# An FNet–GLU layer on one core: x laid out by tiles, early high parts made from raw x, sums and means added by accumulating transfers, and late side work at other places

## The chip, the core and the metric

The kernel runs on one core of a Trainium2 chip. A core has TensorE (PE in the profile: matmuls; PEld is its loading of weights), VectorE (DVE), ScalarE (ACT), GpSimd (POOL) and SyncE (SP). Two queues of transfers matter: SP issues the loads from DRAM ("hardware" transfers), POOL issues the stores and all transfers that add onto their target ("software", accumulating transfers). The metric is the device time of one execution in microseconds (us); a measurement is the median of several runs.

## The reference, cut to what matters

x is [1, 2048, 512], all in fp32.

```python
xn = layernorm(x)                               # over the 512 columns, no weights
a, b = xn @ Dhid_re.T, xn @ Dhid_im.T           # 512 x 512
s = Dseq_re @ a - Dseq_im @ b                   # 2048 x 2048
g = silu((sigmoid(xn @ w_gate) * (xn @ w_up)) @ w_down)   # 512 -> 1792 -> 512
out = x + s * g
```

## The kernel before

**Numbers.** Each fp32 matmul is three TensorE passes over fp32r operands. An operand v is split into a *high* part (ScalarE copies v into an fp32r tile, L118 or L356) and a *low* part (VectorE subtracts the high part from v, L123 or L359); the passes are high·high, high·low and low·high. An operand that takes part in a matmul therefore costs ScalarE about one pass over it and VectorE another.

**Products.** Every large matrix product is done as 2×2 blocks with seven block products instead of eight, which needs sums of blocks (`combine`, L127, on VectorE). For the sequence DFT, the stationary side comes from x (`a_sums`) and the moving side from the DFT matrices (`onto`, L228: t1 = c_re block + c_im block, and so on). Since the real part only is kept, the sequence DFT is made first (real columns of c_re and c_im), and the hidden DFT afterwards.

**Units.** TensorE's work is a list of 245 units in a fixed order. Units 0 to 111 are the sequence DFT: four chunks of 512 output rows (t = 0 to 3), seven products each, four tiles of x (pp = 0 to 3) each, 12 matmuls in a unit. The first 24 units take products 1 and 2 of chunks 0, 1 and 2 in turn, so that one tile of x serves three units: unit 0 needs the first tile, unit 3 the second, unit 6 the third, unit 9 the fourth. Units 112 to 209 are the GLU: 14 blocks of seven units, with 12 matmuls of gate and up and, after the first block, 6 of the down projection. Units 210 to 244 are the hidden DFT, with what was left of the down projection; there silu(g) is multiplied in and the result added onto `out`.

**What sets the order.** The order is written out by hand: `sooner(n, f)`, `amid(n, f)` and `after(n, f)` hang a piece of side work f before, in the middle of, or behind unit n. For each unit the program issues, in this order, the `sooner` work, the loads for this unit and the next five, the high and low parts for this unit and the next two, the `amid` work, the unit's matmuls, the `after` work. Each engine and each queue takes its own instructions in the order in which they are issued.

```python
for k in range(n, min(n + LOAD_AHEAD + 1, len(units))):   # LOAD_AHEAD = 5
    for p in units[k][0]:
        p.load()
ahead = [p for _, (ps, _) in zip(range(SPLIT_AHEAD + 1), units[n:]) for p in ps]   # SPLIT_AHEAD = 2
```

**Pages.** Everything in the core's memory, raw blocks, parts, sums and results alike, lies in 54 pages of 4 KB a partition that are given out in rotation. A new page has to wait until the last reader of its former content is done; where that reader is a store to DRAM, until the store has landed.

**The start** (`begin`, L409). 14 matmuls on a tile of ones run first. x and the first block of c_re come in as two halves each. `stats` (L165) makes mean and variance of a row on VectorE and 1/sqrt(variance + eps) on GpSimd (L175 for 128x1, L178 for 128x2), then −mean on VectorE (L181) and −mean/sigma on GpSimd (L184). `normed` (L351) subtracts and scales on VectorE, `high` copies on ScalarE, `low` subtracts on VectorE. The other half of the columns of a tile is normalised by ScalarE in place (`normalise`, L187). The odd rows of the tiles (j = 1) are treated the same way around units 4 to 16.

**The GLU's x.** The GLU takes a transposed x from the host (x_t) and normalises it in the kernel: `store_moments` (L192) writes −mean and 1/sigma of each block of 512 tokens to DRAM (m_part), and `x_norm` (L462) broadcasts them back to all partitions and, for each of 8 tiles, adds the mean and multiplies by 1/sigma on VectorE (L475, 16 instructions of 128x1024). They hang on units 76 to 97 and 121 to 137.

**Other side work.** `f_sums` (L691) and `w_sums` (L711) make the block sums for the hidden DFT and store them in DRAM (f_sum, w_part). `Seven` holds a GLU block's gated values; its four sums hang on units n+7 to n+10 of a block that begins at n. A block's down projections are stored or added onto g_part in DRAM (`keep`, L515). `put_x` (L737) copies x_t into `out` by seven transfers from DRAM to DRAM, hung on units 40, 48, … 96.

Of the kernel before, what the change touches and what calls it, by code (L numbers as in the profile page):

```python
# [14 lines left out]
P = 128  # L15
# [7 lines left out]
SB = 512  # L23
# [9 lines left out]
def fnet_glu_kernel(ctx: ExitStack, tc: tile.TileContext, x, x_t, c_re, c_im, w_h, w_gu, w_down, out):  # L33
# [18 lines left out]
    nc.gpsimd.memset(mhalf, -0.5)  # L52
    warm = const.tile([P, 2], F32, name="warm")
    nc.scalar.activation(warm, mhalf, AF.Sigmoid)
    moments = const.tile([P, 4, 3, 2, 2], F32, name="moments")
    m_part = [dram.tile([P, 2, 4], F32, name=f"m_part{i}") for i in range(NT)]
# [92 lines left out]
    def fetch(j, pp, e=None):  # L149
        if (j, pp) not in xs:  # L150
            xs[j, pp] = page([2, D], F32)
        if pp == 0:
            rows = x[:SB, :].rearrange("(e j p) d -> j p e d", j=2, e=2)[j]
        else:
            rows = x[pp * SB : (pp + 1) * SB, :].rearrange("(p j e) d -> j p e d", j=2, e=2)[j]
        if e is None and pp:
            nc.sync.dma_start(xs[j, pp], rows)
        else:
            for i in range(2) if e is None else (e,):
                nc.sync.dma_start(xs[j, pp][:, i, :], rows[:, i, :])  # L160

    def moment(pp, m, j):
        return moments[:, 0, m, :, j] if pp == 0 else moments[:, pp, m, j, :]

    def stats(j, pp, apart=None):  # L165
        mv = stat.tile([P, 2, 2], F32, name="mv")
        rs = stat.tile([P, 2], F32, name="rs")
        mean, scale, bias = (moment(pp, m, j) for m in range(3))
        for e in range(2):
# [3 lines left out]
            if apart:  # L173
                nc.vector.tensor_scalar(rs[:, e : e + 1], mv[:, e, 1:2], EPS, None, op0=ALU.add)
                nc.gpsimd.tensor_tensor(scale[:, e : e + 1], rs[:, e : e + 1], mhalf[:, e : e + 1], op=ALU.pow)  # L175
        if not apart:
            nc.vector.tensor_scalar(rs, mv[:, :, 1], EPS, None, op0=ALU.add)
            nc.gpsimd.tensor_tensor(scale, rs, mhalf, op=ALU.pow)  # L178
        if apart:
            apart(mv, 0)  # L180
        nc.vector.tensor_scalar(mean, mv[:, :, 0], -1.0, None, op0=ALU.mult)  # L181
        if apart:
            apart(mv, 1)
        nc.gpsimd.tensor_tensor(bias, mean, scale, op=ALU.mult)  # L184
        return mv
# [6 lines left out]
    def store_moments(b):  # L192
        nc.gpsimd.dma_start(m_part[b], moments[:, b, 0:2].rearrange("p m a b -> p m (a b)"))
# [31 lines left out]
    def c_block(t, pp, j, m):  # L225
        return Load((c_re, c_im)[m][t, j, pp], [2, SB])
# [134 lines left out]
    def prepare(pp, between=None):  # L361
        parts, src = tile_of(pp)

        def step(mv, e):
            normed(pp, mv, e)
            high(parts, src, e)
            if between:
                between(e)
# [594 lines left out]
```

## Time and profile before

| | |
|---|---|
| median of 3 runs | 802.24 us (801.84 to 802.99) |
| the profiled execution | 802.94 us, of which span 801.2 us |
| TensorE clock granted | full in every slice |
| PE busy | 789.2 us (99%), 3470 matmuls |
| DVE busy | 691.5 us (86%), 905 instructions |
| ACT busy | 511.9 us (64%), 783 instructions |
| POOL busy | 118.9 us (15%), 163 instructions |
| transfers | 174.72 MB, mean 218 GB/s |

All times are of one profiled execution. "Busy" is the time that an engine had an instruction in work; matmuls overlap, and a group of n matmuls shown as one row lasts from the start of its first to the end of its last. Behind "<-" stands what an engine had been waiting for. Start times count from the start of the span.

### The profile page before, as it was taken

How to read it: one execution, taken by the hardware profiler on the slowest of the kernel's cores; microseconds unless marked ns; L12 is line 12 of the kernel's file. 1: busy time of each engine (PE TensorE's matmuls, PEld its weight loads, DVE VectorE, ACT ScalarE, POOL GpSimd, SP SyncE). 2: the span in 40 equal slices, each digit the busy share in tenths (PEclk: the TensorE clock that was granted, in tenths of full speed). 3: DMA queues.
4: the chain of work that ended last, by engine and by line, in shares of the span. 5: the costliest groups of instructions: out<-in, count | busy, mean ns of one | idle time of the engine just before them, and what ended most of it. 6: DMA issues, size and time to landing. Idle time of an engine off the chain costs nothing.

```text
span 801.2 us, 9892 instructions
## 1 busy us (share of the span) xinstructions
PE 789.2 (99%) x3470; PEld 649.5 (81%) x3470; DVE 691.5 (86%) x905; ACT 511.9 (64%) x783; POOL 118.9 (15%) x163
## 2 busy tenths in 40 slices
PE   8999999999999999999999999999999999999997
PEld 7787888888878888888887887878888888888886
DVE  7999999688899898899999967869688898896957
ACT  5795655535434455677778776566577787887571
POOL 1321001001110000011111111222131111112201
PEclk9999999999999999999999999999999999999999
DMA  9954065396897336138976885899999798999996
GB/s 337 418 200 174 1 247 200 126 340 233 299 412 296 105 132 213 51 129 220 200 129 92 176 174 169 258 259 243 241 263 214 158 229 224 223 290 300 296 346 106
DMA packets 49617, 174.72 MB, mean 218 GB/s; under 512 B 5536, under 2 KB 5792, under 8 KB 49568
## 3 DMA queue, kind: packets, MB, share of 16 engines
q0 software_dynamic: 20320, 70.28, 40.2%
q1 hardware_dynamic: 29168, 103.76, 35.4%
q8 instruction: 27, 0.44, 0.2%
q14 instruction: 22, 0.18, 0.1%
q10 hardware_dynamic: 80, 0.07, 0.0%
HBM read 106.95 MB, written 70.80 MB: 222 GB/s over the span
## 4 chain that ended last, share of the span: by engine, by line
PE 74%; DVE 13%; issue 5%; DMA 4%; ACT 1%; POOL 1%; SPq 0%; DVEq 0%; POOLq 0%; ACTq 0%
PE pd L70 21%; PE ga L70 13%; PE ua L70 13%; PE gc L70 9%; PE uc L70 9%; DVE page L123 6%; PE gb L70 5%; PE ub L70 5%; DVE page L127 4%; DMA g_part<-page 2%; DMA w_part<-page 2%; DVE page L475 1%; DMA page<-in_c_re_dram 1%; DVE st L171 1%; DVE page L652 1%
## 5 line engine op out<-in xcount | busy, mean ns | idle before, releaser
L118 ACT ACTIVATE page<-page 128x1024 fp32r<-128x1024 f32 (+1 forms) x381 | 301.7, 831 | 153.6 <-DVE page L127 128.8
L123 DVE TENSOR_TENSOR page<-page 128x1024 fp32r<-128x1024 f32 (+1 forms) x381 | 347.1, 943 | 55.9 <-ACT page L118 54.2
L70 PE MATMUL pd<-page 128*128 128x512 f32 (+1 forms) x984 | 238.3, 387 | 0.5 <-ACT page L526 0.5
L70 PEld LDWEIGHTS pd<-page 128*128 128x128 f32 x984 | 183.0, 188 | 38.7 <-ACT page L526 1.0
L127 DVE TENSOR_TENSOR page<-page 128x1024 f32<-128x1024 f32 (+2 forms) x252 | 205.0, 836 | 5.9 <-DMA page<-in_w_gu_dram 5.1
L70 PE MATMUL ga<-page 128*128 128x512 f32 x600 | 156.8, 391 | 4.0 <-DVE page L123 1.8
L70 PE MATMUL ua<-page 128*128 128x512 f32 x600 | 155.5, 389 | 0.0
L70 PEld LDWEIGHTS ga<-page 128*128 128x128 f32 x600 | 112.0, 188 | 30.5 <-ACT page L634 2.7
L70 PEld LDWEIGHTS ua<-page 128*128 128x128 f32 x600 | 112.6, 188 | 23.5
L70 PE MATMUL gc<-page 128*128 128x512 f32 x408 | 106.7, 389 | 0.0
L70 PE MATMUL uc<-page 128*128 128x512 f32 x408 | 106.6, 389 | 0.0
L517 POOL DMA_DIRECT2D g_part<-page x76 | 65.4, 860 | 277.8 <-ACT page L526 160.0
L526 ACT ACTIVATE page<-pd 128x512 f32<-128x512 f32 x140 | 81.8, 600 | 26.2 <-PE pd L70 17.7
L70 PEld LDWEIGHTS gc<-page 128*128 128x128 f32 x408 | 76.5, 188 | 16.1 <-DVE page L123 0.3
L70 PEld LDWEIGHTS uc<-page 128*128 128x128 f32 x408 | 76.6, 188 | 15.9
L70 PE MATMUL gb<-page 128*128 128x512 f32 x228 | 61.1, 390 | 0.2 <-DVE page L123 0.2
L70 PE MATMUL ub<-page 128*128 128x512 f32 x228 | 61.0, 389 | 0.0
L70 PEld LDWEIGHTS gb<-page 128*128 128x128 f32 x228 | 42.6, 188 | 9.6 <-DVE page L123 0.8
L70 PEld LDWEIGHTS ub<-page 128*128 128x128 f32 x228 | 42.8, 188 | 8.9
L294 POOL DMA_DIRECT2D f_raw<-page x16 | 8.7, 542 | 207.1 <-DVE page L306 145.2
L652 DVE TENSOR_TENSOR page<-page 128x512 f32<-128x512 f32 x28 | 19.4, 691 | 8.7 <-ACT page L649 7.9
L612 DVE TENSOR_TENSOR page<-page,pd 128x512 f32<-128x512 f32 x28 | 18.5, 684 | 6.9 <-PE pd L70 6.9
(86 smaller groups left out, 357.2 us busy)
## 6 DMA issues: line engine op xcount, KB each, us to landing
g_part<-page POOLq DMA_DIRECT2D x84, 512.0 KB, 7.1
page<-in_c_re_dram SPq DMA_DIRECT2D x47, 512.0 KB, 8.2
page<-in_c_im_dram SPq DMA_DIRECT2D x32, 512.0 KB, 6.8
page<-f_raw SPq DMA_DIRECT2D x28, 512.0 KB, 8.8
page<-in_w_gu_dram SPq DMA_DIRECT2D x22, 512.0 KB, 6.5
f_raw<-page POOLq DMA_DIRECT2D x16, 512.0 KB, 5.3
f_sum<-page POOLq DMA_DIRECT2D x16, 512.0 KB, 7.2
page<-f_sum SPq DMA_DIRECT2D x16, 512.0 KB, 12.5
```

Of the source, the lines that this page charges most:

```text
L70: nc.tensor.matmul(ps, ws[w], ms[m], start=first and i == 0, stop=last and i == 2, skip_group_check=go_on)
L118: nc.scalar.activation(self.parts[0], self.raw, AF.Copy)
L123: nc.vector.tensor_tensor(lo, self.raw, hi.bitcast(F32), op=SUB)
L127: (engine or nc.vector).tensor_tensor(dst, a, b, op=op)
L171: nc.vector.bn_stats(st, xs[j, pp][:, e, :])
L294: nc.gpsimd.dma_start(f_raw[self.t][block], v)
L475: nc.vector.tensor_tensor(to, to, by, op=(ADD, ALU.mult)[m])
L517: nc.gpsimd.dma_start(g_part[i], pg, accum_op=ADD)
L526: nc.scalar.activation(pg[:, o, :], po, AF.Copy, scale=float(sign))
L612: nc.vector.tensor_add(self.part[:, o, :], self.part[:, o, :], ps)
L652: nc.vector.tensor_mul(s[k][:, 0, :], s[k][:, 0, :], ps["u" + tag] if tag else s[k][:, 1, :])
```

## The change

1. **Layout.** The host lays x out as one contiguous block for each tile and j. The block of tile 0, and the first c_re block of chunks 0 and 1, are laid out as two contiguous halves. The special order of c_re for tile 0 is gone.
2. **Start.** 13 warming matmuls for 14. `normed` is now ScalarE's: for the first half of a tile's columns one instruction makes the high part straight from raw x, and a second one normalises x in place, from which VectorE subtracts the high part; VectorE's subtract-and-scale (L353) and its −mean (L181) are gone. In exchange GpSimd has three small steps for each set of statistics (−mean, power, −mean/sigma) for two. For the third and fourth tile the statistics hang one unit earlier (units 3 and 6) and are made for both rows at once. The order of the matmuls inside units 0 and 3 is another one. `stats(1, pp)` hangs on units 6, 8, 10, 13 (before on 4, 7, 10, 13), its `normalise` on 8, 10, 13, 16 (before 7, 10, 13, 16), and `a_sums` steps 3, 2, 4 on 20+pp, 22+pp, 28+pp (before 10+3pp, 13+3pp, 17+5pp).
3. **Class `Sum`.** For chunk 0, the sums t1 and t3 (eight in all) are not added by VectorE; the c_im block is added onto the loaded c_re or c_im page by an accumulating transfer of POOL's queue.
4. **`x_norm`.** The mean is added onto the raw tile by an accumulating transfer that broadcasts m_part, five units before the multiplication; the raw tile is loaded nine units before it. Only the multiplication is left on VectorE (L501 in the changed kernel, 8 instructions), on units 82, 85, 88, 94 and 122, 125, 129, 132.
5. **Later places.** `w_sums` from unit 158 to 174, `f_sums(1, 1)` from 178 to 182, `put_x` from units 40 to 96 to units 114 to 126, `x_ops(1)` from units 139–150 to 134–150, and the fourth sum of `Seven` from before a unit's loads (n+10) to the middle of unit n+9.

The diff, cut to its core:

```diff
+        def scale(e):
+            mean, by, bias = (moment(pp, m, j)[:, e] for m in range(3))
+            nc.vector.tensor_scalar(rs[:, e], mv[:, e, 1], EPS, None, op0=ALU.add)
+            nc.gpsimd.tensor_tensor(mean, mv[:, e, 0], minus[:, e], op=ALU.mult)
+            nc.gpsimd.tensor_tensor(by, rs[:, e], mhalf[:, e], op=ALU.pow)
+            nc.gpsimd.tensor_tensor(bias, mean, by, op=ALU.mult)
+
             if apart:
-                nc.vector.tensor_scalar(rs[:, e : e + 1], mv[:, e, 1:2], EPS, None, op0=ALU.add)
-                nc.gpsimd.tensor_tensor(scale[:, e : e + 1], rs[:, e : e + 1], mhalf[:, e : e + 1], op=ALU.pow)
+                scale(slice(e, e + 1))
         if not apart:
-            nc.vector.tensor_scalar(rs, mv[:, :, 1], EPS, None, op0=ALU.add)
-            nc.gpsimd.tensor_tensor(scale, rs, mhalf, op=ALU.pow)
-        if apart:
-            apart(mv, 0)
-        nc.vector.tensor_scalar(mean, mv[:, :, 0], -1.0, None, op0=ALU.mult)
-        if apart:
-            apart(mv, 1)
-        nc.gpsimd.tensor_tensor(bias, mean, scale, op=ALU.mult)
-        return mv
+            scale(slice(0, 2))
...
     def store_moments(b):
-        nc.gpsimd.dma_start(m_part[b], moments[:, b, 0:2].rearrange("p m a b -> p m (a b)"))
+        for m in range(2):
+            nc.gpsimd.dma_start(m_part[b][m], moments[:, b, m].rearrange("p a b -> p (a b)"))
...
-        return Load((c_re, c_im)[m][t, j, pp], [2, SB])
+    class Sum(Value):
+
+
+        def __init__(self, base, more):
+            super().__init__([base], None)
+            self.base, self.more = base, more
+
+        def load(self):
+            if self.at is None:
+                self.at = self.base.load()
+                nc.gpsimd.dma_start(self.at, self.more.src, accum_op=ADD)
+
+        def get(self):
+            self.load()
+            return self.at
...
-                t1 = Value([b11, b12], onto(b11.load, b12.load))
+                t1 = Value([b11, b12], onto(b11.load, b12.load)) if t else Sum(b11, b12)
                 t2 = Value([b22], onto(t1.get, b22.load))
-                t3 = Value([b22], onto(b12.load, b22.load))
+                t3 = Value([b22], onto(b12.load, b22.load)) if t else Sum(b12, b22)
...
                 if (self.t, k, pp) == (0, 1, 0):
-                    turns.sort(key=lambda v: v[1])
+                    turns.sort(key=lambda v: (v[1], (0, 2, 1).index(v[2][0])))
+                elif (self.t, k, pp) == (0, 1, 1):
+                    turns.sort(key=lambda v: (v[2] == (2,), v[1], v[2]))
                 elif (k, pp) == (1, 0):
                     turns.sort(key=lambda v: (v[2], v[1]))
...
-            total = (9, 6) if self.t == 0 and k == 5 else (6, 3)
+            total = (9, 3) if self.t == 0 and k in (5, 7) else (6, 3)
...
-    def normed(pp, mv, e):
-        v = a_block(0, 0, pp)[:, e]
-        nc.vector.tensor_scalar(v, v, mv[:, e, 0:1], moment(pp, 1, 0)[:, e : e + 1], op0=SUB, op1=ALU.mult)
+    def normed(pp, to, src, e):
+        nc.scalar.activation(to[:, e], src[:, e], AF.Identity, scale=moment(pp, 1, 0)[:, e : e + 1], bias=moment(pp, 2, 0)[:, e : e + 1])
...
+        for e in range(2):
+            normed(pp, parts[0], src, e)
+        for e in range(2):
+            normed(pp, src, src, e)
...
                     sooner(m - 11, lambda pp=pp: fetch(1, pp))
-                    after(m - 8, lambda pp=pp: stats(1, pp))
-                    after(m - 5, lambda pp=pp: normalise(1, pp))
+                    after((6, 8, 10, 13)[pp], lambda pp=pp: stats(1, pp))
+                    after((8, 10, 13, 16)[pp], lambda pp=pp: normalise(1, pp))
                 else:
                     if pp > 1:
+                        sooner(m - 3, lambda pp=pp: stats(0, pp))
                         sooner(m - 2, units[m][0][1].high)
                         sooner(m - 2, lambda pp=pp: ready.append(prepare(pp)))
                         amid(m - 2, lambda: low(*ready.pop()))
...
-            after(m - 2, lambda pp=pp: a_sums(pp, (3,)))
+            after(20 + pp, lambda pp=pp: a_sums(pp, (3,)))
             after(m - 1, aop[5, pp].get)
-            after(m + 1, lambda pp=pp: a_sums(pp, (2,)))
-            after(m + 5 + 2 * pp, lambda pp=pp: a_sums(pp, (4,)))
+            after(22 + pp, lambda pp=pp: a_sums(pp, (2,)))
+            after(28 + pp, lambda pp=pp: a_sums(pp, (4,)))
...
-            for _ in range((4, 4, 3, 3)[i]):
+            for _ in range((4, 4, 3, 2)[i]):
...
+        first, second = (chunks[t].op[1, 0] for t in range(2))
+        for c in (first, second):
+            c.raw = c.loads[0].at = page([2, SB], F32)
+            c.parts = page([2, SB]), page([2, SB])
+            for e in range(2):
+                nc.sync.dma_start(c.raw[:, e, :], c.loads[0].src[:, e, :])
         fetch(0, 1)
-        for n in (3, 4):
+        for n in (2, 3, 4):
             units[n][0][1].load()
         fetch(0, 2)
         units[5][0][1].load()
-        c.at = page([2, SB]), page([2, SB])
-        a, first = prepare(0, lambda e: high(c.at, raw.at, e))
+        stats(0, 0, True)
+        a, src = tile_of(0)
         for e in range(2):
-            low(a, first, e)
-            low(c.at, raw.at, e)
-        units[1][0][1].get()
+            high(first.parts, first.raw, e)
+            normed(0, a[0], src, e)
+            normed(0, src, src, e)
+            low(first.parts, first.raw, e)
+            low(a, src, e)
+        first.at = first.parts
+        for e in range(2):
+            high(second.parts, second.raw, e)
+        second.get()
+        units[2][0][1].high()
+        stats(0, 1, True)
+        a, src = tile_of(1)
+        normed(1, a[0], src, 0)
+        normed(1, src, src, 0)
         units[2][0][1].get()
+        low(a, src, 0)
         units[3][0][1].high()
-        a, second = prepare(1)
-        low(a, second)
+        normed(1, a[0], src, 1)
+        normed(1, src, src, 1)
+        units[3][0][1].get()
+        low(a, src, 1)
 
...
-        def step(j, m):
+        def centre(j):
+            nc.gpsimd.dma_start(raw[j].load(), mean.unsqueeze(1).to_broadcast([P, 2, SB]), accum_op=ADD)
+
+        def step(j):
             v = xraw[h, j, b] = raw[j].load()
-            by = both.load()[:, :, m, :]
-            if c == 0:
-        sooner(at[0] - 5, both.load)
-        for i in range(4):
-            if i % 2 == 0:
-                sooner(at[i] - 5, raw[i // 2].load)
-            after(at[i], lambda i=i: step(*divmod(i, 2)))
+            nc.vector.tensor_tensor(v, v, by.load().unsqueeze(1).to_broadcast([P, 2, SB]), op=ALU.mult)
+
+        sooner(at[0] - 5, by.load)
+        for j in range(2):
+            sooner(at[j] - 9, raw[j].load)
+            after(at[j] - 5, lambda j=j: centre(j))
+            after(at[j], lambda j=j: step(j))
...
             for i, v in enumerate(self.sums):
-                sooner(n + 7 + i, v.get)
+                (amid if i == 3 else sooner)(n + (7, 8, 9, 9)[i], v.get)
...
         n = len(units)
-        x_norm(0, 0, (n - 36, n - 33, n - 30, n - 27))
-        x_norm(0, 1, (n - 24, n - 21, n - 18, n - 15))
+        x_norm(0, 0, (n - 30, n - 27))
+        x_norm(0, 1, (n - 24, n - 18))
...
-        x_norm(1, 0, (n + 9, n + 12, n + 15, n + 18))
-        x_norm(1, 1, (n + 21, n + 22, n + 24, n + 25))
-        x_ops(1, (n + 27, n + 28, n + 29, n + 30, n + 31, n + 32, n + 33, n + 34, n + 35, n + 36, n + 38))
+        x_norm(1, 0, (n + 10, n + 13))
+        x_norm(1, 1, (n + 17, n + 20))
+        x_ops(1, (n + 22, n + 24, n + 26, n + 27, n + 28, n + 30, n + 32, n + 33, n + 35, n + 36, n + 38))
-        f_sums(1, 1, n + 66, 1)
-        w_sums(n + 46)
+        f_sums(1, 1, n + 70, 1)
+        w_sums(n + 62)
+        for i, (pair, k) in enumerate(itertools.product(range(NT // 2), BLOCK)):
+            if (pair, k) != LAST:
+                after(n + 2 + 2 * i, lambda pair=pair, k=k: put_x(pair, *BLOCK[k]))
```

In the rows below, `ga`, `ua` and so on are accumulators in PSUM, `page` is any page, `st`, `mv`, `rs` and `moments` hold the statistics, and the number behind an L is the line of the kernel that the rows are of (L123 and L127 before are L125 and L129 in the changed kernel, L171 is L178, L359 is L376).

VectorE at the third tile of x (needed by unit 6), from its statistics to its low part, before:

```order
L171 BN_STATS st<-page 128x6
L172 BN_AGGR mv<-st 128x2
L174 TENSOR_SCALAR rs<-mv 128x1
L353 TENSOR_SCALAR page<-page,mv,moments 128x256
L181 TENSOR_SCALAR moments<-mv 128x2
L353 TENSOR_SCALAR page<-page,mv,moments 128x256
L123 TENSOR_TENSOR page<-page 128x1024
L359 TENSOR_TENSOR page<-page 128x512
```

and in the changed kernel (the row of `rs` is L171 there):

```order
L178 BN_STATS st<-page 128x6
L179 BN_AGGR mv<-st 128x2
L171 TENSOR_SCALAR rs<-mv 128x2
L125 TENSOR_TENSOR page<-page 128x1024 x2
L376 TENSOR_TENSOR page<-page 128x512
L125 TENSOR_TENSOR page<-page 128x1024
```

Between the statistics and the low part stand two subtractions of other operands now, one before; the two L353 are gone from VectorE.

GpSimd at the same tile and the next set of statistics, before:

```order
L175 TENSOR_TENSOR moments<-rs,mhalf 128x1 x2
L184 TENSOR_TENSOR moments<-moments 128x2
L178 TENSOR_TENSOR moments<-rs,mhalf 128x2
L184 TENSOR_TENSOR moments<-moments 128x2
```

and in the changed kernel, for one set, with the first transfers that follow the last set:

```order
L172 TENSOR_TENSOR moments<-mv,minus 128x2
L173 TENSOR_TENSOR moments<-rs,mhalf 128x2
L174 TENSOR_TENSOR moments<-moments 128x2
L192 DMA m_part0a<-moments 128x4
L192 DMA m_part0b<-moments 128x4
L238 DMA page<-in_c_im_dram 128x1024 x3
```

Three steps stand where two or three stood, and the accumulating transfers of `Sum` (L238) share the queue with the stores of the moments.

VectorE around units 76 to 82, before (L306 is `join`, L475 is `x_norm`):

```order
L475 TENSOR_TENSOR page<-page 128x1024
L127 TENSOR_TENSOR page<-page 128x1024
L123 TENSOR_TENSOR page<-page 128x1024
L127 TENSOR_TENSOR page<-page 128x1024 x2
L123 TENSOR_TENSOR page<-page 128x1024
L127 TENSOR_TENSOR page<-page 128x1024
L123 TENSOR_TENSOR page<-page 128x1024
L306 TENSOR_TENSOR page<-page,pd 128x512 x2
L475 TENSOR_TENSOR page<-page 128x1024
L127 TENSOR_TENSOR page<-page 128x1024 x2
L123 TENSOR_TENSOR page<-page 128x1024 x2
```

and in the changed kernel (`join` is L324, the multiplication L501):

```order
L125 TENSOR_TENSOR page<-page 128x1024
L324 TENSOR_TENSOR page<-page,pd 128x512 x2
L129 TENSOR_TENSOR page<-page 128x1024 x2
L125 TENSOR_TENSOR page<-page 128x1024 x2
L129 TENSOR_TENSOR page<-page 128x1024
L125 TENSOR_TENSOR page<-page 128x1024
L501 TENSOR_TENSOR page<-page 128x1024
```

The two L475, the additions of unit 76 and the multiplication of unit 79, are gone from this place; the first multiplication stands behind unit 82, at the end of these rows.

71 lines of the change are left out of this document (28 added, 43 removed).

## The prediction

> **What bounds the kernel now.** I read the page first.
>
> ```profile
> PE 789.2 (99%) x3470; PEld 649.5 (81%) x3470; DVE 691.5 (86%) x905; ACT 511.9 (64%) x783; POOL 118.9 (15%) x163
> PE 74%; DVE 13%; issue 5%; DMA 4%; ACT 1%; POOL 1%; SPq 0%; DVEq 0%; POOLq 0%; ACTq 0%
> ```
>
> TensorE is busy for 99% of the span, and the change takes one of the warming matmuls from it and nothing else. Only 801.2 − 789.2 = 12 us of the span are without a matmul: the time before the first one, the last store, and waits in between. The next view is the list of what PE waited for.
>
> ```profile
> PE ga L70 <- DVE page L123: 1.8, 1, 1.8
> PE ga L70 <- ACT page L634: 1.3, 2, 0.8
> PE ga L70 <- ACT page L356: 0.6, 1, 0.6
> PE pd L70 <- ACT page L526: 0.5, 1, 0.5
> PE ga L70 <- DVE page L359: 0.3, 1, 0.3
> PE gb L70 <- DVE page L123: 0.2, 1, 0.2
> ```
>
> Beside the first matmul's (the 0.6) these are 4.1 us in six waits. A wait costs more than its row; PE's timeline shows it for the longest.
>
> ```profile
> 230.74 1.52 PE L70 MATMUL ua<-page 128*128 128x512 f32 x6
> 232.10 0.61 PE L70 MATMUL ga<-page 128*128 128x512 f32 x2
> 234.47 1.20 PE L70 MATMUL ga<-page 128*128 128x512 f32 x4 [1.76 <-DVE page L123]
> 235.51 1.54 PE L70 MATMUL ua<-page 128*128 128x512 f32 x6
> ```
>
> Six matmuls take 232.10 − 230.74 = 1.36 us, 0.227 each; a unit of 12 takes 2.72, a GLU unit of 18 takes 4.08. From 232.10 to 234.47 are 2.37 us for two matmuls (0.45), so 1.92 are lost, and the four behind them take 1.04 for 0.91, 0.13 more. The wait of 1.76 cost 2.05, that is 0.28 above its row.
>
> **Where the waits come from.** First VectorE ahead of this one, and the window's busy times (PE, PEld, DVE, ACT, POOL; then clock, DMA share, GB/s).
>
> ```profile
> 217.72 2.10 DVE L475 TENSOR_TENSOR page<-page 128x1024 f32<-128x1024 f32 x1
> 228.89 2.13 DVE L475 TENSOR_TENSOR page<-page 128x1024 f32<-128x1024 f32 x1
> 233.21 2.42 DVE L123 TENSOR_TENSOR page<-page 128x1024 fp32r<-128x1024 f32 x2
> ```
>
> ```profile
> 220.00:240.00 20.00, 18.24 (x81) 14.77 (x80) 20.00 (x18) 6.93 (x8) 2.87 (x5) 1.00 1.02 412
> ```
>
> VectorE had no free moment in this window (20.00 of 20.00), and PE was released when the first of the two subtractions ended. Two additions or multiplications of `x_norm` (4.23 us) had been put in ahead of it. It is a backlog of VectorE, not a missing load. Then ScalarE in the GLU, and two steps of the chain of waits there:
>
> ```profile
> 434.99 0.63 ACT L118 ACTIVATE page<-page 128x512 fp32r<-128x512 f32 x1 [2.55 <-issue]
> 493.93 0.60 ACT L634 ACTIVATE page<-ga 128x512 f32<-128x512 f32 x1 [0.63 <-DVE page L123]
> 526.17 1.09 ACT L526 ACTIVATE page<-pd 128x512 f32<-128x512 f32 x2 [2.47 <-DMA w_part<-page]
> ```
>
> ```profile
> 480.15 7.06 DMA g_part<-page
> 513.72 12.37 DMA w_part<-page
> ```
>
> At 435 ScalarE stood for 2.55 us, and its snapshot of PSUM (L634), for which PE waits, came behind it. I put that to VectorE, which was busy there with `x_norm`'s last instructions and the sums of `x_ops(1)`. At 494 and 526 a page was still on its way to DRAM when ScalarE wanted to fill it again: behind the loads of `w_sums` (unit 154 on) a store of g_part took 7.06 us, and the store of w_part 12.37.
>
> **The sum, part by part.**
>
> *Middle of the kernel: −4.7 us.* Of the two L475 ahead of 233.21 one addition is gone altogether and one multiplication stands behind unit 82, the unit that waited; VectorE has 4.2 us less to do there and was 1.9 late. In the second stretch, eight instructions become four and stand from unit 122 to 132 instead of 121 to 137; `w_sums` leaves units 154 to 161. So all four waits go: 1.8 + 1.3 + 0.5 from the list and 4 × 0.28 = 1.1 for the restarts, 4.7. The bounds are −2.0 (only the wait at 234) and −4.7.
>
> *What pays for it.* Each mean is now an accumulating transfer. The rows are the landing of the nearest such group (accumulations onto g_part, L517), and the loads of x_t around 200 to 260 us:
>
> ```profile
> DMA to landing us min/median/max: 5.1/7.2/15.0
> ```
>
> ```profile
> page<-in_x_t_dram SPq DMA_DIRECT2D x4, 512.0 KB, 7.6
> ```
>
> Raw load and accumulation follow each other, 14.8 us by the medians; from the load, nine units ahead, to the multiplication are 9 × 2.72 = 24.5 us. Hidden, so nothing; with the longest landing 22.6 us, and it still holds. The seven copies of `put_x` leave the sequence DFT, which makes room on the same transfer engines.
>
> *Sums of chunk 0: nothing by themselves.* Eight additions leave VectorE:
>
> ```profile
> L127 DVE TENSOR_TENSOR page<-page 128x1024 f32<-128x1024 f32 x76 | 92.3, 1221 | 0.0
> ```
>
> 8 × 1.22 = 9.8 us. The transfers are issued nine units ahead of their own unit and the split begins two units ahead, so there are 7 × 2.72 = 19 us; t1 only accumulates (7.2, at most 15.0), t3 loads first (14.8 together, 22.6 with the longest). Taken as hidden; the bound is 3.6 us once.
>
> *Start: −0.6 us.* The rows of GpSimd's power and multiplication, the first matmul, and ScalarE's normalisation of half a tile:
>
> ```profile
> 4.82 0.57 POOL L175 TENSOR_TENSOR moments<-rs,mhalf 128x1 f32<-128x1 f32 x1 [3.98 <-DVE rs L174]
> 6.49 0.20 POOL L184 TENSOR_TENSOR moments<-moments 128x2 f32<-128x2 f32 x1
> 7.01 0.50 PE L70 MATMUL ga<-page 128*128 128x512 f32 x1 [0.62 <-ACT page L356]
> ```
>
> ```profile
> L190 ACT ACTIVATE page<-page,moments 128x256 f32<-128x256 f32 x8 | 4.3, 593 | 0.0
> ```
>
> First matmul: 4.82 + 0.20 + 0.57 + 0.20 + 0.59 and 0.1 of handing on give 6.5 for 7.01, −0.5. In the second half of unit 0 ScalarE has two normalisations and one copy to do again, some 1.6 us for 1.36 of matmuls, and VectorE a subtraction behind them: +0.4. The second tile waits for the same chain once more, +0.2 (0 to 1.3). For the third tile:
>
> ```profile
> 19.41 0.69 DVE L171 BATCH_NORM_STATS2 st<-page 128x6 f32<-128x512 f32 x1
> 23.73 0.68 DVE L359 TENSOR_TENSOR page<-page 128x512 fp32r<-128x512 f32 x1
> 24.33 0.69 DVE L171 BATCH_NORM_STATS2 st<-page 128x6 f32<-128x512 f32 x1
> 26.07 0.17 DVE L177 TENSOR_SCALAR rs<-mv 128x2 f32<-128x2 f32 x1
> 52.28 2.96 DVE L123 TENSOR_TENSOR page<-page 128x1024 fp32r<-128x1024 f32 x3
> ```
>
> ```profile
> 26.32 1.67 POOL L178 TENSOR_TENSOR moments<-rs,mhalf 128x2 f32<-128x2 f32 x1 [3.81 <-DVE moments L181]
> 52.39 1.17 POOL L184 TENSOR_TENSOR moments<-moments 128x2 f32<-128x2 f32 x1
> ```
>
> Before, from statistics to low part took 24.41 − 19.41 = 5.0 us. Now: both rows' statistics 26.24 − 24.33 = 1.9; three steps of GpSimd; four activations of ScalarE, 4 × 0.54 = 2.1 (4.3 / 8 of the row above); the subtraction 0.69. GpSimd's multiplication takes 0.20 alone and took 1.17 while VectorE ran its subtractions (it ended at 53.56, as the first of the three at 52.28 did): it is held by them. So its three steps take from 0.20 + 2 × 0.57 + 0.20 = 1.5 us to 1.17 + 1.67 + 1.17 = 4.0, and the order puts two subtractions right behind the statistics. The chain makes 6.2 to 8.7 for 5.0; it begins a unit (2.72) earlier. That leaves −1.5 to +1.0; I take +0.5, nearer the upper end, because the subtractions stand at that very place. [...] The fourth tile:
>
> ```profile
> 32.60 0.63 PE L70 MATMUL ua<-page 128*128 128x512 f32 x2
> 33.55 0.73 PE L70 MATMUL ga<-page 128*128 128x512 f32 x2 [0.32 <-DVE page L359]
> ```
>
> 0.95 for two matmuls that take 0.45, 0.8 lost there with the pairs beside it; its statistics now start a unit earlier, and the additions that crowded VectorE come later: −0.6. The 0.2 of the list (at 70.4, 0.6 with what follows it) was VectorE's backlog, and 9.8 us are gone: −0.6. In all −0.5 + 0.4 + 0.2 + 0.5 − 0.6 − 0.6 = −0.6, from −2.3 (nothing given back, the later tiles as now or better) to +1.3 (second tile 1.3, third 1.0).
>
> *`w_sums` at its new place: +0.8 us.* Now it is at units 170 to 177, where these stand:
>
> ```profile
> 560.00:580.00 20.00, 20.00 (x90) 16.57 (x89) 12.31 (x18) 11.56 (x20) 3.40 (x4) 1.00 0.93 248
> 580.00:600.00 20.00, 20.00 (x90) 16.57 (x89) 16.12 (x23) 14.76 (x27) 6.46 (x9) 1.00 1.00 252
> 600.00:620.00 20.00, 20.00 (x90) 16.57 (x89) 17.16 (x29) 15.62 (x27) 3.20 (x4) 1.00 0.95 218
> ```
>
> PE loses nothing there today (20.00), but the transfer engines have little left. In the rotation of pages, the changed program reuses at units 168 to 169 pages that were sent to DRAM only two units (8.2 us) before; the closest ones of before were one to three units, at units 155 to 164, where it cost the two waits. A store lands in 7.2 us by the median and 15.0 at most: 0 to 2.2 us (what the two waits at 494 and 526 cost), and I take 0.8, since two units are more than the median.
>
> *Without effect on the end:* the layout as such (the loads are ahead of their use except the first), the fourth sum of `Seven` (moved by half a unit behind loads that it doesn't feed), `f_sums(1, 1)` four units later, with its first use tens of units away, and the last store, which is unchanged.
>
> Sum: −4.7 − 0.6 + 0.8 = −4.5. The profiled execution took 802.94 us (span 801.2), 0.7 above the median; I take the difference from the median: 802.24 − 4.5 = **797.7 us**. Its own range: −4.7 − 2.3 = −7.0 gives 795.2, and −4.7 + 1.3 + 2.2 = −1.2 gives 801.0.
>
> **Rivals.**
>
> *The means land late.* Raw load and accumulation run in the stretch where the transfer engines are full (1.02 in the window above), and 10 + 15 = 25 us are past the 24.5. VectorE then stands at L501 in order, with the subtractions for PE behind it; the wait at 234 stays (2.05): 799.8. Against it: only the longest landings reach this. 12%.
>
> *Slower: `w_sums` in the full stretch.* Eight transfers of 512 KB, at 412 GB/s 1.27 us each, make 10.2 us; free in the three windows are (0.07 + 0.00 + 0.05) × 20 = 2.4. The other 7.8 are passed on to loads and stores, ScalarE waits for pages, and PE for ScalarE: 797.7 + 7.8 = 805.5 at most. It decides from 4.5 us on. For it: no share is free and pages come back after two units. Against it: loads run five units (20 us) ahead, so a delay of 8 us is hidden unless it is a page's. 12%.
>
> *The start eats it.* If GpSimd is held in all steps of all four tiles, the second and third give +2.3 and the gains on the fourth and at 70 stay away: −0.6 becomes +2.3, 802.24 − 4.7 + 2.3 + 0.8 = 800.6. For it: the two blocked rows. 10%.
>
> *It doesn't do what it says.* The waits at 436, 494 and 526 have another cause, and the freed one at 234 turns up behind the next instructions (VectorE has fewer of them, but stays the fullest engine beside PE): 802.2. 8%.
>
> **How the numbers follow.** Forecast 58%, rivals 12, 12, 10 and 8. A difference under 0.2% (1.6 us: 800.6 to 803.8) can't be told from none. Faster: the forecast (0.56 of it), the late means (0.10), half of the start, part of the slower rival: 0.74. Slower: most of that rival and tails of the last two, 0.12. The same: 0.14. The range of 795.2 to 801.7 holds the forecast, the late means, the start, and a `w_sums` that passes on up to half of its 7.8 us; what is left out is the rest of that rival and the case in which nothing changes.
>
> **What would show it.** Right: no L634 or L526 in PE's list around 436 to 530, no wait at 234, first matmul near 6.5, GpSimd's steps above 1 us at the third tile with a small wait of PE at unit 6, and one short page wait at 550 to 570. Wrong: VectorE idle before L501 for a transfer; waits of ScalarE for g_part or w_part at 550 to 600 of over 2 us in the list; PE waiting over 1 us at unit 3 or 6.

## The result, and the profile after

The changed kernel takes 801.13 us (median of 16 runs, 799.03 to 802.04), the kernel before 802.52 (16 runs, 801.22 to 803.83): ratio 0.998, 95% interval 0.9972 to 0.9988. It is faster by 1.4 us; 4.5 were forecast. The time is inside the range; the gain is less than a third of what was predicted.

The page of the changed kernel, busy times and the chain that ended last by engine:

```profile
PE 789.0 (99%) x3469; PEld 650.0 (81%) x3469; DVE 669.0 (84%) x872; ACT 519.4 (65%) x792; POOL 141.0 (18%) x194
PE 90%; DMA 5%; DVE 2%; ACT 1%; issue 1%; POOL 0%; SPq 0%; DVEq 0%; ACTq 0%
```

VectorE has 22.5 us less to do, and the chain runs through TensorE for 90% (74% before); its next share is transfers, where it was VectorE. What PE still waits for, beside the warming matmuls:

```profile
PE pd L72 <- DVE page L125: 1.3, 3, 0.7
PE ga L72 <- DVE page L376: 0.7, 1, 0.7
PE gc L72 <- ACT page L120: 0.7, 1, 0.7
PE gc L72 <- DVE page L125: 0.5, 1, 0.5
PE ga L72 <- ACT page L370: 0.4, 1, 0.4
```

All waits of the GLU are gone, and so is the 1.8 at 234 us. The rows of 1.3, 0.7 (L120) and 0.5 are new, and they stand close together in PE's timeline:

```profile
246.53 0.73 PE L72 MATMUL gc<-page 128*128 128x512 f32 x2 [0.69 <-ACT page L120]
247.79 1.20 PE L72 MATMUL gc<-page 128*128 128x512 f32 x4 [0.53 <-DVE page L125]
251.19 3.06 PE L72 MATMUL pd<-page 128*128 128x512 f32 x12 [0.38 <-DVE page L125]
254.96 5.78 PE L72 MATMUL pd<-page 128*128 128x512 f32 x24 [0.71 <-DVE page L125]
260.93 2.56 PE L72 MATMUL pd<-page 128*128 128x512 f32 x10 [0.19 <-DVE page L125]
```

Lost time is counted here as in the prediction: from start to start of the matmuls, less 0.227 us each, so a wait's restart is in it (0.28 us at 234 in the kernel before).

| place in the program | lost before | lost after | change | forecast |
|---|---|---|---|---|
| first matmul begins at | 7.01 | 7.00 | 0.0 | −0.5 |
| unit 0 | 0.1 | 0.6 | +0.5 | +0.4 |
| second tile (17 us) | 0.2 | 0.2 | 0.0 | +0.2 |
| third tile (unit 6, 26 us) | 0 | 1.0 | +1.0 | +0.5 |
| fourth tile (33 us) | 0.8 | 0 | −0.8 | −0.6 |
| 70 to 74 us | 0.6 | 0 | −0.6 | −0.6 |
| 234 us | 2.0 | 0 | −2.0 | −2.0 |
| **246 to 261 us** | 0 | **3.9** | **+3.9** | **0** |
| 436, 488 to 529 us | 3.0 | 0 | −3.0 | −2.7 |
| 540 to 620 us | 0 | 0 | 0 | +0.8 |

The spans are 801.2 and 799.8; the changes add up to −1.0, and the rest of the 1.4 lies in differences below 0.02 us a matmul. The one row that wasn't forecast at all is the largest. The other rows come near their sum (−4.9 for −4.5), in part by luck: the start is 0.7 worse than forecast, and the row of 540 to 620 us 0.8 better. At 246 to 261 us, VectorE and ScalarE of the changed kernel:

```profile
246.51 1.22 DVE L125 TENSOR_TENSOR page<-page 128x1024 fp32r<-128x1024 f32 x1 [2.39 <-ACT page L120]
252.54 1.23 DVE L129 TENSOR_TENSOR page<-page 128x1024 f32<-128x1024 f32 x1 [1.40 <-DMA page<-in_c_im_dram]
255.11 1.22 DVE L129 TENSOR_TENSOR page<-page 128x1024 f32<-128x1024 f32 x1 [0.20 <-DMA page<-in_c_im_dram]
```

```profile
245.42 2.01 ACT L120 ACTIVATE page<-page 128x1024 fp32r<-128x1024 f32 x2 [4.20 <-DMA page<-in_c_re_dram]
```

Neither is behind with its work; both stand and wait for blocks of the DFT matrices. The windows around it, first before, then after (columns as in the prediction):

```profile
240.00:250.00 10.00, 10.00 (x46) 8.29 (x45) 10.00 (x9) 4.48 (x6) 1.77 (x3) 1.00 1.03 420
250.00:260.00 10.00, 10.00 (x45) 8.27 (x45) 10.00 (x9) 5.00 (x6) 0.00 (x0) 1.00 0.46 188
260.00:270.00 10.00, 10.00 (x46) 8.27 (x45) 10.00 (x10) 5.28 (x7) 0.00 (x0) 1.00 0.15 52
```

```profile
240.00:250.00 10.00, 8.78 (x38) 6.63 (x37) 6.98 (x7) 3.07 (x3) 2.28 (x3) 1.00 1.06 350
250.00:260.00 10.00, 8.90 (x38) 6.67 (x37) 8.39 (x9) 4.38 (x6) 1.22 (x1) 1.00 1.04 391
260.00:270.00 10.00, 9.81 (x44) 7.80 (x43) 10.00 (x10) 6.88 (x8) 0.00 (x0) 1.00 0.28 49
```

Before, VectorE is full and the transfer engines have room in the second of the windows. After, VectorE is free for nearly a quarter of the first two, and the transfer engines are full in both: (1.06 + 1.04 + 0.28) × 10 = 23.8 us of their time for 16.4. The landings (us from issue to arrival, the last number) from 200 to 260 us, before and after:

```profile
page<-in_c_im_dram SPq DMA_DIRECT2D x8, 512.0 KB, 8.6
```

```profile
page<-in_c_im_dram SPq DMA_DIRECT2D x8, 512.0 KB, 16.8
page<-m_part0a POOLq DMA_DIRECT2D x2, 512.0 KB, 13.2
page<-m_part1a POOLq DMA_DIRECT2D x2, 512.0 KB, 9.6
```

The c_im blocks take twice as long. They aren't issued later: the last four leave SP's queue from 240.1 to 247.9 us, before from 239.6 to 247.7. Their landings, before and after:

```profile
DMA to landing us min/median/max: 6.9/9.1/10.0
```

```profile
DMA to landing us min/median/max: 13.5/15.4/17.5
```

The last c_re block, issued at 229.4 us (before 227.3), took 16.0 us for 8.1. So most of the time went into the transfers, not into waiting for pages ahead of them.

### The profile page after: what moved, and what is told of

Its sections match the earlier page's. It is cut to its first block, busy times and chain, and to the rows that moved or that the text cites. A ratio compares the mean times of both kernels' runs of the same rounds, so it can differ in the third digit from the quotient of the medians.

```text
span 799.8 us, 9917 instructions
## 1 busy us (share of the span) xinstructions
PE 789.0 (99%) x3469; PEld 650.0 (81%) x3469; DVE 669.0 (84%) x872; ACT 519.4 (65%) x792; POOL 141.0 (18%) x194
## 3 DMA queue, kind: packets, MB, share of 16 engines
q0 software_dynamic: 23776, 78.67, 44.6%
## 4 chain that ended last, share of the span: by engine, by line
PE 90%; DMA 5%; DVE 2%; ACT 1%; issue 1%; POOL 0%; SPq 0%; DVEq 0%; ACTq 0%
PE pd L72 25%; PE ga L72 16%; PE ua L72 16%; PE gc L72 11%; PE uc L72 11%; PE ub L72 6%; PE gb L72 6%; DMA page<-in_c_im_dram 3%; DMA page<-f_raw 2%; DVE page L125 1%; ACT page L370 1%; DMA page<-in_c_re_dram 1%; DVE page L129 0%; POOL moments L173 0%; DVE st L178 0%
## 5 line engine op out<-in xcount | busy, mean ns | idle before, releaser
L125 DVE TENSOR_TENSOR page<-page 128x1024 fp32r<-128x1024 f32 (+1 forms) x381 | 347.0, 941 | 72.9 <-ACT page L120 69.7
L120 ACT ACTIVATE page<-page 128x512 fp32r<-128x512 f32 (+1 forms) x380 | 299.7, 831 | 121.1 <-DVE page L129 91.0
L129 DVE TENSOR_TENSOR page<-page 128x1024 f32<-128x1024 f32 (+2 forms) x244 | 195.4, 820 | 3.2 <-DMA page<-in_c_im_dram 2.0
L72 PEld LDWEIGHTS gb<-page 128*128 128x128 f32 x228 | 42.8, 188 | 8.9
L72 PEld LDWEIGHTS ub<-page 128*128 128x128 f32 x228 | 42.8, 188 | 8.9
L660 ACT ACTIVATE page<-ga 128x512 f32<-128x512 f32 x28 | 16.6, 594 | 20.0 <-PE ga L72 18.2
```

Of the source, the lines that this page charges most:

```text
L72: nc.tensor.matmul(ps, ws[w], ms[m], start=first and i == 0, stop=last and i == 2, skip_group_check=go_on)
L120: nc.scalar.activation(self.parts[0], self.raw, AF.Copy)
L125: nc.vector.tensor_tensor(lo, self.raw, hi.bitcast(F32), op=SUB)
L129: (engine or nc.vector).tensor_tensor(dst, a, b, op=op)
L660: nc.scalar.activation(s[k][:, m, :], ps[c + "a"], AF.Copy)
```

## The experiments

Two theories for the new wait. **A**: the accumulating transfers of the mean use transfer engines that are full here already, and the loads beside them come late. **B**: the multiplications stand at a wrong place in VectorE's order. "Lost" is all of PE's lost time behind the first matmul, in the profiled execution (before 6.8, changed 5.7). It is one execution: e1 lost 0.9 us at 91 us, far ahead of the place of its edit, where the changed kernel lost nothing, so a difference of that size between two profiles says little by itself. The ratios are to the kernel before in the same job, 802.86 for e1 to e4, 802.65 for e5 to e8 and 803.14 for e9 to e12; beside the changed kernel (801.13, with 802.52 before) medians of other jobs are good to about 0.6 us.

| | median us | ratio to before (95%) | lost | of it 246–261 |
|---|---|---|---|---|
| e1 no accumulated mean | 797.82 | 0.9936 (0.9922–0.9951) | 2.5 | 0 |
| e2 mean by VectorE | 799.07 | 0.9952 (0.9938–0.9965) | 3.3 | 0 |
| e3 f_sums(0, 1) later | 797.81 | 0.9937 (0.9923–0.9951) | 2.7 | 0 |
| e4 put_x back | 802.82 | 0.9997 (0.9985–1.0008) | 6.3 | 4.8 |
| e5 e3 and start | **796.19** | **0.9919** (0.9905–0.9932) | 0.6 | 0 |
| e6 w_sums back | 802.17 | 0.9996 (0.9985–1.0007) | 5.5 | 3.5 |
| e7 means earlier | 803.12 | 1.0004 (0.9995–1.0013) | 6.9 | 0 |
| e8 e3, mean by VectorE | 798.66 | 0.9949 (0.9937–0.9961) | 3.1 | 0 |
| e9 e6 and Seven back | 802.08 | 0.9993 (0.9982–1.0003) | 5.9 | 3.1 |
| e10 before, w_sums later | 801.72 | 0.9987 (0.9976–0.9997) | 6.0 | 0 |
| e11 e10, f_sums(0, 1) later | 799.34 | 0.9956 (0.9942–0.9971) | 3.3 | 0 |
| e12 sums by VectorE | 802.44 | 0.9995 (0.9983–1.0007) | 5.4 | 2.1 |

**e1: without the accumulated mean.**

```diff
-            after(at[j] - 5, lambda j=j: centre(j))
+            after(at[j] - 5, lambda j=j: raw[j].load())
```

> The changed kernel without the eight accumulating transfers of the mean (L497; x_t is only multiplied, so the GLU's x lacks its mean). Theory A (the accumulating transfers take too much of the transfer engines where these are full already, so that the loads of the DFT matrices come late): PE's five waits between 246 and 261 us, 3.9 us of lost time in the changed kernel, shrink to under 1 us, the loads of c_im there land in about 10 us instead of 16.8, and the median is about 3.5 us below the changed kernel's, 797.5. Theory B (the multiplications stand at the wrong place in VectorE's order): the waits stay above 2.5 us and the median within 1 us of 801.1.

The waits are gone, and the median is 3.3 us below the changed kernel's. The landings from 200 to 262 us:

```profile
page<-in_c_im_dram SPq DMA_DIRECT2D x8, 512.0 KB, 11.2
```

B falls: VectorE's order is unchanged in e1. That VectorE stood at a multiplication for a late mean, which e1 would have mended too, is ruled out by the changed kernel's profile: no idle time stands before any of its eight L501. The software queue's share of the transfer engines, before, changed and e1:

```profile
q0 software_dynamic: 20320, 70.28, 40.2%
```

```profile
q0 software_dynamic: 23776, 78.67, 44.6%
```

```profile
q0 software_dynamic: 21600, 74.47, 42.8%
```

44.6% of 799.8 us less 42.8% of 796.5 is 15.8 us for eight transfers: 2.0 us of all 16 engines each. The sixteen that the change added cost 356.7 − 322.1 = 34.6, 2.2 each.

**e2: the mean by VectorE again.** `x_norm` as before, with two loads for the two halves of m_part, on units 76 to 97 and 121 to 132.

> The changed kernel with the mean added by VectorE again, at the places of before in the first half (units 76 to 97) and on units 121 to 132 in the second. Theory A: the waits at 246 to 261 go (3.9 us), and VectorE's backlog brings a wait near 234 back, up to 2.05 us; the median is 799 to 801. Theory B: the same waits would not appear either, so this run prices the trade only: if it is below 801.1, the accumulating mean costs more than it saves.

799.07, 2.1 us *faster* than with the transfers. At 234 only 0.2 us were lost, not 2.05, with as many instructions ahead of that place on VectorE as before. The two of `x_norm` had become shorter; in e2 they are

```profile
218.09 1.22 DVE L499 TENSOR_TENSOR page<-page 128x1024 f32<-128x1024 f32 x1
228.37 1.22 DVE L499 TENSOR_TENSOR page<-page 128x1024 f32<-128x1024 f32 x1
```

where the prediction's rows have 2.10 and 2.13. Of the sixteen instructions of the kernel before, only the four of the first 512 tokens took 2.1 us, the others 1.22; those four alone took the mean and 1/sigma in a turned order, which the new layout of x made needless. That is 1.8 us less ahead of a wait that cost 2.05. In the GLU 1.0 us is lost at 424 to 434, where before lost 0.8 at 436: there the accumulated mean does save something.

**e3: f_sums(0, 1) out of the stretch.**

```diff
-        f_sums(0, 1, n - 35, 2)
+        f_sums(0, 1, n + 40, 1)
```

> The changed kernel with f_sums(0, 1), four loads and four stores of 512 KB, moved from units 77 to 83 to units 152 to 155; the means stay accumulating transfers. Theory A: eight transfers fewer (about 10 us of the transfer engines) in the full stretch, so the waits between 246 and 261 us (3.9 us) fall under 1 us and the median to about 797.5. Theory B: they stay above 2.5 us. In both the eight transfers may cost up to 1 us at their new place.

797.81; no loss at 246 to 261, with all transfers of the mean in place. A holds from a second side, though e3 also takes four additions from VectorE there, which wasn't behind. At the new place 0.9 us are lost, at 462 to 491, as allowed for.

**e4: put_x back.**

```diff
-                after(n + 2 + 2 * i, lambda pair=pair, k=k: put_x(pair, *BLOCK[k]))
+                after(40 + 8 * i, lambda pair=pair, k=k: put_x(pair, *BLOCK[k]))
```

> The changed kernel with the seven copies of x_t into out back at units 40 to 96; three of them fall into 205 to 250 us. Theory A: three more transfers in the full stretch, each 1.3 to 2.5 us of the transfer engines, so PE's waits there grow from 3.9 to 7 to 11 us and the median to 804 to 808. Theory B: no change beyond 1 us.

802.82: 1.7 us above the changed kernel, and 1.2 under the least that theory A gave. c_im landed in 18.9 us for 16.8, but in the profile PE's waits did not grow: of the 4.8 us lost, 1.6 are matmuls at half clock (ten from 260.08 to 264.06 us, 3.98 for 2.27; see the last section), and the other 3.2 are less than the changed kernel's 3.9. From 200 to 262 us POOL's queue had 43.9% of the transfer engines, in the changed kernel 39.1%: 3.0 us more, about 1 us for each of the three copies, under the 1.3 to 2.5 that was expected. So a fuller stretch alone doesn't say how long PE waits.

**e5: e3, with the start mended.**

```diff
         for e in range(2):
+            if e == 0:
+                normed(0, a[0], src, e)
             high(first.parts, first.raw, e)
-            normed(0, a[0], src, e)
+            if e:
+                normed(0, a[0], src, e)
...
-                        sooner(m - 3, lambda pp=pp: stats(0, pp))
+                        sooner(m - (4, 3)[pp - 2], lambda pp=pp: stats(0, pp))
```

> The kernel of e3 with two edits at the start. (1) ScalarE normalises the first half of the first tile before it copies the first half of c_re, not behind it. If c_re's landing at 5.6 to 6.3 us and the order on ScalarE set the first matmul (7.0 to 7.4 in the five kernels with the changed start), it comes 0.5 us earlier; if the statistics set it, nothing changes. (2) The third tile's statistics hang one unit earlier (unit 2). If their late begin (18.9 us, not the 16.7 that I counted with) and the chain behind it set PE's wait at unit 6 (0.98 us lost in all five), the wait falls under 0.2; if it is only that GpSimd is held by VectorE's subtractions, more of them stand behind the statistics now and 0.6 or more stays. By the first halves 797.8 - 0.5 - 0.9 = 796.4.

796.19, the best of all, 0.8% under the kernel before, with 0.6 us lost behind the first matmul. The third tile in the changed kernel, VectorE and GpSimd:

```profile
18.91 0.69 DVE L178 BATCH_NORM_STATS2 st<-page 128x6 f32<-128x512 f32 x1
20.73 2.37 DVE L125 TENSOR_TENSOR page<-page 128x1024 fp32r<-128x1024 f32 x2
25.30 0.69 DVE L376 TENSOR_TENSOR page<-page 128x512 fp32r<-128x512 f32 x1 [2.20 <-ACT page L370]
```

```profile
20.89 1.62 POOL L173 TENSOR_TENSOR moments<-rs,mhalf 128x2 f32<-128x2 f32 x1
22.60 0.55 POOL L174 TENSOR_TENSOR moments<-moments 128x2 f32<-128x2 f32 x1
```

and VectorE in e5:

```profile
16.71 0.69 DVE L178 BATCH_NORM_STATS2 st<-page 128x6 f32<-128x512 f32 x1
23.09 0.69 DVE L376 TENSOR_TENSOR page<-page 128x512 fp32r<-128x512 f32 x1 [0.98 <-ACT page L370]
```

The chain is 25.99 − 18.91 = 7.1 us in the one and 7.1 in the other; it begins 2.2 us earlier, and the 1.0 us at unit 6, lost in every other kernel with the changed start, is 0. The late begin of the chain set it. That the first matmul (6.68) gained by the exchange is not shown: it came between 6.35 and 7.44 in the other ten kernels with the changed start, a spread wider than the gain.

**e6 and e9: w_sums back, then Seven's fourth sum too.**

```diff
-        w_sums(n + 62)
+        w_sums(n + 46)
...
-                (amid if i == 3 else sooner)(n + (7, 8, 9, 9)[i], v.get)
+                sooner(n + 7 + i, v.get)
```

> The changed kernel with w_sums back on unit 158. If its loads and stores made the two waits for pages at 494 and 526 us of before, these come back (2.0 us between them) and the median is about 803; waits between 246 and 261 stay. If the waits had another cause (VectorE's work, the sums of Seven), the median stays within 0.8 us of 801.1.

> The kernel of e6 with the fourth sum of Seven also back ahead of unit n+10. e6 gave 802.17 and only 0.4 us of lost time around 494, not the 2.0 of before. If Seven's place was the other half, PE's waits at 494 and 526 lose 1.5 to 2.2 us again and the median is about 803.3; if not, it stays at e6's 802.2 within 0.8 us.

1.0 us slower than the changed kernel each, and only 0.4 and 0.7 us lost in the GLU. The store behind w_sums' loads takes about as long as before (7.06):

```profile
478.74 8.10 DMA g_part<-page
```

but ScalarE's wait for it reaches PE for 0.36 us at 494, not 1.12.

**e7: the first half's means 12 units earlier.**

```diff
-        x_norm(0, 0, (n - 30, n - 27))
-        x_norm(0, 1, (n - 24, n - 18))
+        x_norm(0, 0, (n - 42, n - 39))
+        x_norm(0, 1, (n - 36, n - 30))
```

> The changed kernel with x_norm of the first half 12 units earlier (multiplications behind units 70, 73, 76, 82), so that the accumulating transfers of the mean begin at about 190 us, where the transfer engines are about half busy, and end before c_im's loads. Theory A: the waits between 246 and 261 us (3.9 us) shrink to under 1.5 us, and the median is 798 to 799.5, since VectorE has the multiplications ahead of the stretch in which it was late before. If only the number of bytes in the whole stretch counts and not when they come, the waits stay above 2.5 us.

Not as expected: c_im's landings are good (7.8 us), nothing is lost at 246 to 261, and yet it is the slowest, with 5.0 us lost from 204 to 237:

```profile
PE ga L72 <- ACT page L317: 1.5, 1, 1.5
PE ga L72 <- DVE page L125: 1.4, 2, 1.1
PE pd L72 <- DVE page L125: 0.5, 1, 0.5
```

It brings the accumulations next to the first f_sums (the transfer engines' share is 1.09 from 190 to 200 us), and the loads of SP's queue, which stood still from 196 to 204 us in its timeline, come late behind them. Whether the accumulations or the standstill of SP's queue made most of it was not tried.

**e8: e3 with the mean by VectorE.**

> The kernel of e3 with the mean added by VectorE as in e2. If the accumulating mean is worth its 4.9 us of VectorE's time once the transfer engines have room, this is slower than e3's 797.8 by 1 us or more; if VectorE's backlog at 234 was as much f_sums' four additions, it is the same within 0.8 us.

798.66, 0.85 above e3, between the two expectations and not clear of noise (the intervals overlap). The profiles don't show the difference, with spans of 797.0 and 797.2: e8 loses 1.1 us at 424 to 434, in the GLU, and e3 loses 0.9 at 462 to 491, each where the other loses nothing. At 234 and at 246 to 261 nothing is lost in either. There the accumulated mean was worth nothing once four additions of f_sums were away.

**e10 and e11: the kernel before, with w_sums at its new place, then f_sums(0, 1) too.**

> The kernel before with w_sums alone moved to unit 174. If its transfers made both waits for pages, those at 494 and 526 us are gone, those at 234 (2.05 us) and 436 (0.77) stay, no new one comes at 550 to 620, and the median is 2.0 us lower, about 800.6. If it is half the cause, about 801.6.

> The kernel of e10 with f_sums(0, 1) moved from units 77 to 83 to 152 to 155 as in e3; means and the start as before. If the wait at 234 is VectorE's backlog, three additions fewer (3.7 us) ahead of it remove it as well as the accumulating mean was meant to, and no wait comes at 246 to 261: about 798.6, with up to 0.9 us lost at 460 to 490. If the wait there is not a matter of how much VectorE has to do, it stays near 2 us.

e10: no wait from 488 to 529 (2.2 us lost there before), the waits at 436 and 234 as they were, none new; 1.4 us faster than the kernel before beside it (803.14). e11: 799.34, nothing lost at 234 and nothing at 246 to 261. Two lines changed in the kernel before give 3.8 us, against 1.4 for the whole change.

**e12: chunk 0's sums by VectorE.** `Sum` isn't used; the three lines concerned are as before.

> The changed kernel with the eight sums of chunk 0 added by VectorE again. If the accumulating sums are what took the waits at 70 to 73 us away (0.6 us), these come back and the median rises by 0.6 or more, to about 801.7; if the transfers cost as much as the additions (a wait of up to 0.9 us at 91 stood in e1 and e2, behind a late c_im), it stays within 0.4 us of 801.1.

802.44, 1.3 us above the changed kernel. The waits did not come back at 70 to 74 but at 96 to 104 (2.0 us lost). So the accumulating sums seem to pay, by about what was expected of them; this is no more than likely, since the ratios to the kernel before (0.9995 and 0.998) have intervals that overlap, and the profile loses 1.8 us less at 246 to 261, which nothing here explains.

## Why the prediction was wrong

**The step that failed** is in the sum, "What pays for it": "Hidden, so nothing", and "`put_x` … makes room on the same transfer engines". I worked out whether an accumulated mean would land in time for its own multiplication, and left out what the transfer takes from the loads beside it. It did land in time, more narrowly than I had it: the accumulation has the last five of those nine units, 13.6 us, and the first two took 13.2 by the median. I had quoted the row that spoke against it, a share of 1.02 at 220 to 240 us. Each accumulation takes 2.0 us of the transfer engines. Four came into the stretch and three copies of `put_x` left it, which wasn't room enough: from 200 to 270 us the transfer engines were busy for 59.6 us, before 54.5, and from 240 on for 7.4 us more. PE lost 3.9. With e1 and e3 the cause is shown twice, and both are 5.0 us below the kernel before of their job (802.86). How much of such a load reaches PE isn't settled: in its profile e4 has three transfers more and no more waiting.

**The rival came near and named another path.** "The means land late" had VectorE stand at the multiplication. The full transfer engines were its premise, and that was right; the loads of c_re and c_im were the ones that came late, and VectorE never stood at L501.

**234 us, −2.0: right**, but not for the mean alone. e2 loses 0.2 there with VectorE adding the mean, e11 nothing with three additions of f_sums moved. It was a backlog, and about 2 us taken from it were enough. "Without effect on the end: the layout as such" was wrong here: by e2, the layout's shorter `x_norm` instructions took nearly all of this wait away without any accumulating transfer.

**GLU, −2.7: right, −3.0.** e10 gives w_sums' part, 2.2. The 0.8 at 436 goes with VectorE's means of the second half, by e2, e8 and e10; e9 lost 0.4 there without them. Open: why w_sums put back (e6) costs the changed kernel only 0.4 us of lost time there; Seven's sum is not the reason (e9).

**`w_sums` at its new place, +0.8: nothing.** No wait from 540 to 620 us, and the rival on the slower side, which passed on 7.8 us there, was wrong with it: the transfer engines were as full as it said (1.02, 1.06 and 0.96 in its three windows), but PE had no wait. The same reasoning would have been right at 240 us, where I didn't use it.

**The start, −0.6: +0.1.** GpSimd's steps were as long as bounded (power 1.62, multiplication 0.55), and the chain of 7.1 us lay within 6.2 to 8.7. Wrong was "it begins a unit earlier": it began 0.5 us earlier (18.91 for 19.41), since the subtractions ahead of it on VectorE wait for ScalarE:

```profile
17.77 1.23 DVE L125 TENSOR_TENSOR page<-page 128x1024 fp32r<-128x1024 f32 x1 [0.52 <-ACT page L120]
```

And the first matmul didn't gain 0.5. In this profile ScalarE waited for c_re until 5.83 us, with the normalisation queued behind; whether that set it is not shown (e5):

```profile
5.83 0.63 ACT L373 ACTIVATE page<-page 128x512 fp32r<-128x512 f32 x1 [3.59 <-DMA page<-in_c_re_dram]
6.37 1.22 ACT L370 ACTIVATE page<-page,moments 128x256 fp32r<-128x256 f32 x2
```

## What to carry to other kernels

Work that is moved from an engine to a transfer is priced in the stretch where it lands: add its time on the transfer engines (2.0 us for each accumulation here) to their share there, and ask which loads stand beside it, not only whether it arrives in time itself. Before a busy engine's work is handed over, look for work in the same stretch that nobody needs soon; here moving four additions with their eight transfers (e11 against e10, 2.4 us) did more than the whole rewrite (1.4). When one edit of several shortens an instruction, look whether it already does what another is meant for (2.1 to 1.22 us for `x_norm`'s first four, here). Where a step is issued earlier, ask whether what stands ahead of it on its engine is waiting: the third tile's statistics, issued a unit (2.72 us) earlier, began 0.5 us earlier, behind a subtraction that waited 0.52 for ScalarE.

## What the runs showed of the hardware

In e10's profile a wait of about 2 us cost nearly twice its length. After 1.95 us lost at 234.8 us, the next matmuls ran at about half speed:

```profile
234.81 1.42 PE L70 MATMUL ga<-page 128*128 128x512 f32 x4 [1.79 <-DVE page L123]
236.03 2.76 PE L70 MATMUL ua<-page 128*128 128x512 f32 x6
238.59 1.75 PE L70 MATMUL ga<-page 128*128 128x512 f32 x6
```

Eight matmuls took 0.427 us each for 0.227, 1.6 us more, and the granted clock (the third number from the end) was half in just this stretch. Below are e10 and then the kernel before, which with 1.92 lost at the same place went on at full speed:

```profile
235.60:239.00 3.40, 3.40 (x9) 2.64 (x8) 3.40 (x4) 1.00 (x2) 0.56 (x1) 0.50 1.03 423
```

```profile
235.50:239.00 3.50, 3.50 (x17) 2.88 (x16) 3.50 (x4) 1.32 (x2) 0.56 (x1) 1.00 1.03 420
```

e4 paid it after 2.27 us lost at 260 (clock 0.51 from 260.2 to 263.6); e7, with 1.62 at most, did not. So the half clock came after waits of about 2 us (1.95 and 2.27 lost), but not after each of them (1.92), and what makes the difference is not shown. It goes with part of the spread: of e10's twelve executions the six with a mean clock of 0.996 or 0.997 took 802.13 to 803.39 us, the six at 0.999 or 1.0 took 800.32 to 801.31. The four of e5, without a wait of that length, took 795.9 to 797.0; but the twelve of e6, with no clock under 0.998, spread from 800.71 to 804.5, so it isn't the whole of it. For kernels that differ by 1 us, such a wait (1.95 us and 1.6 behind it in e10) is the first thing to remove.
